# A sparse-attention and expert kernel: one small load moved ahead of K, three table loads moved to GpSimd's queue, one more unit transposed by TensorE

## The chip, the cores and the metric

The kernel runs on one core of a Trainium2 chip. The metric is the device time of one execution in microseconds (us). TensorE (PE) multiplies, VectorE (DVE) and ScalarE (ACT) do elementwise work, GpSimd (POOL) does elementwise work and issues gathers and scatters, and SyncE (SP) issues most transfers. Each engine takes its instructions strictly in the order of the program; the engines wait for one another by semaphores.

## What is computed

Block-sparse attention over 4 batches, 8 heads, 768 positions in 24 blocks of 32, followed by a mixture of 8 experts that gives each of the 3072 tokens to one expert:

```python
for qb in range(n_blocks):
    for kb in sampled_blocks[qb]:                 # 3 sampled blocks of a query block
        mask[qb*block:(qb+1)*block, kb*block:(kb+1)*block] = True   # beside window, first, last
attn = softmax(where(mask, q @ k.T / sqrt(D), -1e9));  x = attn @ v
e_idx = argmax(x @ w_gate, axis=1)                # the expert of each token
for e in range(E):
    mask = e_idx == e
    h  = np.maximum(x[mask] @ w1[e], 0.0)         # [*, 512] @ [512, 1024]
    out[mask] = gate_w[mask, None] * eom[mask, e, None] * (h @ w2[e])
```

## The kernel before

**Setup.** SP's queue opens with the two halves of K (`load_k`, L383), then six loads of V (L386). ACT's queue opens with the first tile of q and then `setup_load` (L184): the 72 sampled block numbers, broadcast to 128 partitions (`raw`). From `raw`, GpSimd marks repeated blocks (`setup_dup`, L217 to L227) and VectorE works out the gather indices `vidx` (`setup_blocks`, L314 to L351). VectorE's program has `setup_blocks` ahead of its first reduction over scores (`mx0d`, L563), GpSimd's has `setup_dup` ahead of the scaled copies of K (`fixed` L400, `gather_k` L422).

**Attention.** 52 units of work (4 dense and 22 sparse for each of two batch pairs) run as a software pipeline: in each step PE does the scores of one unit (L555 or L491), the transposes of another (L455), the output product of a third (L588 or L524 and L531).

**Experts.** Tokens are routed while attention still runs. Expert work is cut into units. Units 0 to 4 ("early") start before all tokens are known. Then a plan on VectorE and GpSimd (`plan`, L791 to L865) writes the table `es` with expert and first table row of the planned units, numbered from 5. Their kinds are, from unit 5 on, P P M P P M P M P M S S: P has 256 tokens, S 128, M 32. For each unit SP reads registers from `es` (`load_g`, L920 and L922), loads the unit's rows of the token table (`load_t`, L937 for M, L940 for P and S, which also waits for the 24 scatters that fill the table) and its weights in eight pieces of 512 KB (`load_w`, L948); GpSimd gathers the tokens (`load_x` L969, `m_load` L1107) and scatters results (`store_y`, L1095). Pieces live in three sets of buffers used in turn, so units 7 and 8 reuse those of units 4 and 5. A table tile is reused after four units, once the stores that read it have landed.

**Turning x.** PE needs x with the 512 features on partitions. For units in `PEX` (0 to 5) PE transposes it (L999), ACT writes the high half (L1000) and VectorE the low half (`x_l`, L1006). For the others ACT and VectorE split x first (`x_s`, L979 and L980), and SP's queue transposes it by DMA (L994).

**Order.** A hand-written schedule gives every piece of work a step and a rank inside it (`program`); the order of the ranks is the order on every engine. A step of the expert stage is about one group of 12 matmuls (L1045, `p_h`) and one of 6 (L1077, `p_y`). `first(u, j)` is the step from which piece j of unit u may be loaded. Unit 4 starts at step 32, unit 5 at 40, unit 6 at 48; unit 7 multiplies at steps 54 to 56, unit 8 starts at 56.

Of the kernel before, what the change touches and what calls it, by code (L numbers as in the profile page):

```python
# [15 lines left out]
ET = mybir.EngineType  # L16

B, H, S, D = 4, 8, 768, 64
NB, BLK = 24, 32
# [7 lines left out]
EMPTY = E * LS  # L27
# [6 lines left out]
NE = 5  # L34
NOWN = NE - 1
# [28 lines left out]
EARLY_X = (28, 29), (36, 36), (38, 39), (48, 49), (53, 54)  # L64
# [13 lines left out]
FIRST = PER + ND + 1  # L78
# [9 lines left out]

PEX = tuple(range(NE + 1))
PARTS = (5, 5, 4), (5, 5)

KC = (("act", 3, (0,)), ("pool", 3, (1, 2)), ("pool", 2, (3, 4, 5)))
# [18 lines left out]
def tile_kernel(ctx, tc, q, k, v, sampled, wg, wcat, out):  # L113
    nc = tc.nc
# [66 lines left out]

    def setup_load():
        src = sampled.bitcast(I32).rearrange("a c -> (a c)").rearrange("(o n two) -> o n two", o=1, two=2)
        nc.scalar.dma_start(raw, src.to_broadcast([128, NB * 3, 2]))  # L184

    setp = ExitStack()
    sp = setp.enter_context(tc.tile_pool(name="setup", bufs=1))
# [584 lines left out]
    def after_scatters(i, n=NT):  # L772
        for name in scattered[:n]:
            tc.add_manual_dep(
                i, name, mybir.DependencyInfo(mybir.DependencyClass.Sync, mybir.DependencyReason.DATA),
                reason="table")
# [140 lines left out]
    def load_g(u):  # L917

        w = u - NE
        _, regs[u] = nc.values_load_multi_w_load_instructions(  # L920
            es[w:w + 1, 0:2], engines=[ET.SP], min_val=0, max_val=E - 1)
        rows[u], = nc.values_load_multi_w_load_instructions(  # L922
            es[w:w + 1, 2:3], engines=[ET.SP], min_val=0, max_val=EMPTY)[1]

    def load_t(u):
        m = 1 if KIND[u] == "M" else 2
        tabs[u] = rt.tile([128, m, TW], I32, tag=f"tab{m}", name=f"tab{u}", bufs=4)
        m = tiles_of(u)
        if u < NE:
            src = table[ds(regs[u][1], 128 * m)].rearrange("(p m) c -> p m c", m=m)  # L930
            after_scatters(nc.sync.dma_start(tabs[u][:, 0:m], src).ins, RG[OF[u]][1])
            return
        assert len(scattered) == NT
        if KIND[u] == "M":

            src = table[ds(rows[u], 32)].rearrange("(o p) c -> o p c", o=1).to_broadcast([4, 32, TW])
            after_scatters(nc.sync.dma_start(tabs[u][:, 0], src).ins)  # L937
            return
        src = table[ds(rows[u], 128 * m)].rearrange("(p m) c -> p m c", m=m)
        after_scatters(nc.sync.dma_start(tabs[u][:, 0:m], src).ins)  # L940

    def load_w(n):
        u, j = n // 8, n % 8
# [324 lines left out]
    def program(n0, n1):  # L1268
# [13 lines left out]
        def first(u, j):  # L1282

            if u < NE + 2:
                return (30, 34)[u - NE] + j // 2
            v = u - 3
            return POS[v] + 1 + j // 4 if KIND[v] == "M" else POS[v] + j - 2

        for u in range(NUNIT):
            t = POS[u]  # L1290
            small = KIND[u] == "M"
            if u >= NE:
                later = end + u - NE
                get = max(min(t - 28, first(u, 0)), later)
                do(get, 0, load_g, u)
                for j in range(NFC):
                    do(max(first(u, j), get), 0.6, load_w, NFC * u + j)
                do(max(t - 18, later), 0.5, load_t, u)
            if small:
                do(max(t - 16, later + 1), 1, m_load, u)  # L1300

                for d, rank, f in ((-4, 9.5, m_x), (-3, 7.5, m_xc), (-2, 9.5, m_h), (-1, 7.5, m_hc), (-1, 9.5, m_t),
                                   (0, 7.5, m_tc), (0, 9.5, m_y), (1, 7.5, m_o), (2, 13, m_store)):
                    do(t + d, rank, f, u)
                continue
            if u >= NE:
                for m in range(2):
                    do(max(t - 16, later + 1), 1, load_x, 2 * u + m)
                do(max(t - 10, later + 3), 13, x_s, u)
            for m in range(2):  # L1310
                x = max(t - 2 + m, EARLY_X[u][m] + 1 - FIRST) if u < NE else t - 3 + m if u in PEX else t - 8
                do(x, 15, x_t, 2 * u + m)
                do(x + 1 if u < NE else x, 3 if u < NE else 16, x_l, 2 * u + m)
            yl = LAG(u, 7) + 1
            do(t + 7 + yl, 4 if u < NOWN else 12, y_o, u)
            for m in range(2):
                do(t + 8 + yl + (m if u < NOWN else 0), 13, store_y, 2 * u + m)
            e = u < NOWN
            lead = 2 if e else 3
            for j in range(NFC):  # L1320
                n, p = NFC * u + j, t + j
                do(p - lead, 6, w_h, n)
                do(p - lead, 7, w_l, n)
                if e:

                    do(max(p - 5, (-3, 5, 5, 15)[u]), 0.6, load_w, n)
                elif u < NE:
                    do(p - 10, 0.6, load_w, n)
                do(p, 8, p_h, n)
                do(p + LAG(u, j), 9, p_y, n)  # L1330
                if j % 2 == 1:
                    do(p if u < NE else p + 1, 10, h_h, n // 2)
                    do(p + 1, 2 if u < NE else 11, h_l, n // 2)
# [134 lines left out]
```

## Time and profile before

| | |
|---|---|
| median of three runs | 585.51 us (585.29 to 586.24) |
| the profiled execution | 588.49 us, its span 586.7 us |
| PE busy | 519.2 us (89% of the span), 7373 matmuls |
| DVE, ACT, POOL busy | 354.6, 314.2, 242.2 us |
| TensorE clock granted, mean | 0.956 of full speed |
| DMA | 138.67 MB, mean 236 GB/s |

PE is the busiest engine. The share is an average: it is near full in the second half of the expert stage and lower in the first 40 us and where the expert units follow one another around 370 to 430 us. In a row of the timeline the columns are start, duration, engine, line, operation, tiles, shapes and count; in brackets stands how long the engine was idle before it and what ended that. An engine's name with a q is its sequencer (SPq: a transfer is issued).

### The profile page before, as it was taken

The page shows a single profiled execution, that of the slowest core. Times are in us where ns is not written, and L with a number is a line of the kernel's source. Part 1 is how long each engine was busy: PE and PEld are TensorE (multiplying, and loading weights), DVE is VectorE, ACT ScalarE, POOL GpSimd, SP SyncE. Part 2 cuts the span into 40 slices and gives each one's busy share as a digit, 9 for nine tenths or more (in the row PEclk, how much of TensorE's full clock was granted, in tenths as well). Part 3 has the DMA queues.
Part 4 walks back from the last instruction along what each step waited for, and adds up shares of the span by engine and source line. Part 5 has one row for each costly group of instructions (what it writes and reads, how often), then busy time and mean ns, then how long its engine had stood idle before and what let it go on. Part 6 is the DMA issues. An engine that isn't in the chain of part 4 may idle for free. (4 is left out here: it accounts for less than half of the span.)

```text
span 586.7 us, 18727 instructions
## 1 busy us (share of the span) xinstructions
PE 519.2 (89%) x7373; PEld 361.5 (62%) x7373; DVE 354.6 (60%) x730; ACT 314.2 (54%) x583; POOL 242.2 (41%) x366
## 2 busy tenths in 40 slices
PE   4389889897888989999998999896899999999994
PEld 3157666565556657676765666574567666766772
DVE  2677657575657647776763567656366474555571
ACT  1165656565556647577674546355375455455470
POOL 2853644743560783817837007420322303312111
PEclk8599989999998989999999899898989999999998
DMA  8955979794398459776865376399998999976111
GB/s 313 305 169 187 331 228 302 229 324 110 79 298 274 143 172 336 237 223 198 254 196 194 94 286 235 139 384 408 287 347 309 299 405 312 288 245 221 24 39 35
DMA packets 60481, 138.67 MB, mean 236 GB/s; under 512 B 21663, under 2 KB 28319, under 8 KB 60128
## 3 DMA queue, kind: packets, MB, share of 16 engines
q1 hardware_dynamic: 48896, 100.57, 53.3%
q0 software_dynamic: 11200, 36.48, 20.1%
q8 instruction: 60, 0.98, 0.7%
q10 hardware_dynamic: 288, 0.34, 0.2%
q14 instruction: 37, 0.30, 0.2%
HBM read 128.05 MB, written 14.81 MB: 244 GB/s over the span
## 5 line engine op out<-in xcount | busy, mean ns | idle before, releaser
L1045 PE MATMUL h<-xb,kr 128*128 128x256 f16 (+1 forms) x780 | 90.7, 267 | 10.0 <-ACT xb L1000 4.8
L1045 PEld LDWEIGHTS <-kr 128*128 128x128 f16 x780 | 71.0, 100 | 30.7 <-issue 12.5
L1077 PE MATMUL S<-kr,hh 128*128 128x512 f16 x348 | 86.2, 382 | 0.0
L422 POOL TENSOR_TENSOR kr<-kn,eighth 128x256 f32<-128x256 f32 x110 | 68.5, 649 | 19.4 <-issue 9.4
L498 DVE TENSOR_REDUCE mx<-S 128x4 f32<-128x1024 f32 x44 | 53.7, 1221 | 35.4 <-PE S L491 19.2
L506 ACT ACTIVATE P<-S,mx 128x256 f32<-128x256 f32 x176 | 69.3, 483 | 9.4 <-DVE mx L498 6.5
L458 ACT COPY pt<-T 128x512 f32<-128x512 f32 x66 | 36.6, 589 | 46.4 <-PE T L455 41.8
L439 POOL DMA_INDIRECT vt<-in_v_dram,vidx x44 | 47.6, 1083 | 29.1 <-PE O L524 23.0
L1077 PEld LDWEIGHTS <-hh 128*128 128x128 f16 x384 | 37.3, 99 | 31.2 <-issue 1.2
L491 PE MATMUL S<-kr,qall 64*32 64x256 f32 x1408 | 50.9, 394 | 1.4 <-issue 1.4
L1058 ACT ACTIVATE hh<-h 128x512 f16<-128x512 f32 (+1 forms) x36 | 19.8, 549 | 60.4 <-PE h L1045 59.2
L1031 DVE SCALAR_TENSOR_TENSOR kr<-e,kr 128x1024 f16<-128x1024 f32 x32 | 38.7, 1226 | 19.1 <-ACT kr L1027 14.7
L455 PE MATMUL T<-ident,P 128*128 128x128 f32 x352 | 48.6, 281 | 0.7 <-issue 0.7
L455 PEld LDWEIGHTS T<-ident,P 128*128 128x128 f32 x352 | 41.7, 148 | 2.1 <-issue 1.4
L524 PE MATMUL O<-vt,pt 128*32 128x65 f32 x1408 | 34.5, 222 | 8.7 <-issue 8.3
L531 PE MATMUL O<-vc,pt 128*64 128x65 f32 x704 | 33.7, 229 | 6.6 <-issue 6.5
L969 POOL DMA_INDIRECT xb<-xscr,tab x16 | 16.4, 1027 | 53.6 <-PE O L1045 14.6
L765 POOL DMA_INDIRECT table<-vals,place x24 | 26.0, 1085 | 28.8 <-DVE vals L716 15.0
L524 PEld LDWEIGHTS O<-vt,pt 128*32 128x32 f32 x1408 | 26.5, 109 | 18.3 <-issue 12.9
L1064 DVE SCALAR_TENSOR_TENSOR hh<-h,hh 128x512 f16<-128x512 f32 (+1 forms) x36 | 22.6, 627 | 21.8 <-ACT hh L1058 21.8
L1095 POOL DMA_INDIRECT out_dram<-yo,tab x16 | 17.6, 1101 | 42.4 <-ACT yo L1088 33.9
L491 PEld LDWEIGHTS S<-kr,qall 64*32 64x32 f32 x1408 | 22.2, 108 | 19.8 <-issue 10.5
(342 smaller groups left out, 981.1 us busy)
## 6 DMA issues: line engine op xcount, KB each, us to landing
e<-in_wcat_dram SPq DMA_DIRECT2D x80, 512.0 KB
rk<-in_wcat_dram SPq DMA_DIRECT2D x30, 512.0 KB
vc<-in_wcat_dram SPq DMA_DIRECT2D x14, 512.0 KB
vn<-in_v_dram SPq DMA_DIRECT2D x12, 520.0 KB
xscr<-x SPq DMA_DIRECT2D x48, 128.0 KB
qall<-in_q_dram SPq DMA_DIRECT2D x23, 256.0 KB
vc<-in_v_dram SPq DMA_DIRECT2D x22, 260.0 KB
ws<-in_wcat_dram SPq DMA_DIRECT2D x8, 512.0 KB
```

What stands on the lines that cost most here:

```text
L422: nc.gpsimd.tensor_tensor(r[:, slot], kn[bp][:, ds(rv, 1)].rearrange("p o n -> p (o n)"), eighth.to_broadcast([128, 256]), op=ALU.mult)
L439: nc.gpsimd.indirect_dma_start(vt[bp, i][:, s].rearrange("p b j w -> p (b j w)"), None, v, bass.IndirectOffsetOnAxis(ap=vidx[:, bp, i, s:s ...
L455: nc.tensor.transpose(pt[:, 128 * c:128 * c + 128], p[:, 128 * c:128 * c + 128], ident)
L458: nc.scalar.copy(t[:, 0:w], pt[:, 0:w])
L491: nc.tensor.matmul(s[64 * h2 + 32 * qi:64 * h2 + 32 * qi + 32, b, hp], t[p, 64 * j + 32 * qi:64 * j + 32 * qi + 32], g[p, 1 - qi:3:1 + qi, ...
L498: nc.vector.tensor_reduce(mx, self.s.rearrange("p b h n -> p (b h) n"), axis=AX.X, op=ALU.max, negate=True)
L506: nc.scalar.activation(p[:, 256 * hp:256 * hp + 256], self.s[:, b, hp], AF.Exp, bias=self.mx[:, 2 * b + hp:2 * b + hp + 1])
L524: nc.tensor.matmul(o[row:row + 32, b, hp, 0:VW], self.t[b][:, col:col + 32], av[:, qi, b, 4 * h2 + 2 * hg + hp], start=b == 0 and hp == 0, ...
L531: nc.tensor.matmul(o[64 * h2:64 * h2 + 64, b, hp, 0:VW], self.t[b][:, col:col + 64], cv[:, b, 4 * h2 + 2 * hg + hp], start=False, stop=b = ...
L1031: nc.vector.scalar_tensor_tensor(w[:, 1], piece(n), SW, w[:, 0], op0=ALU.mult, op1=ALU.subtract)
L1045: nc.tensor.matmul(hps[n // 2][:, cols(n)], w[:, hl, 128 * c:128 * c + 128], x[:, xl, c], start=cnt == 0, stop=cnt == 11)
L1077: nc.tensor.matmul(y, a[:, k], w[:, l, 512:1024], start=n % 8 == 0 and cnt == 0, stop=n % 8 == 7 and cnt == 2)
```

## The change

`setup_load` moves from ACT's queue to SP's, where it stands ahead of the two loads of K. For units 5, 6 and 7 the first-row register is read on GpSimd and `load_t` is issued from GpSimd's queue. `PEX` takes in unit 6, so its x is transposed by PE and no longer split by `x_s` and transposed by DMA. `x_t` of unit 4 stands one step earlier (29 and 30 for its two halves), that of unit 5 one step later (38 and 39); unit 6's stands at 46 and 47. The pieces of unit 7 are loaded from steps 41 to 48 on (34 to 37 before), those of unit 8 from 43 to 50 (38 to 45 before).

```diff
+POOLT = NE + 3
-PEX = tuple(range(NE + 1))
+PEX = tuple(range(NE + 2))
 def setup_load():
-        nc.scalar.dma_start(raw, src.to_broadcast([128, NB * 3, 2]))
+        nc.sync.dma_start(raw, src.to_broadcast([128, NB * 3, 2]))
 def load_g(u):
-            es[w:w + 1, 2:3], engines=[ET.SP], min_val=0, max_val=EMPTY)[1]
+            es[w:w + 1, 2:3], engines=[ET.Pool if u < POOLT else ET.SP], min_val=0, max_val=EMPTY)[1]
 def load_t(u):
+        queue = nc.gpsimd if u < POOLT else nc.sync
-            after_scatters(nc.sync.dma_start(tabs[u][:, 0], src).ins)
+            after_scatters(queue.dma_start(tabs[u][:, 0], src).ins)
-        after_scatters(nc.sync.dma_start(tabs[u][:, 0:m], src).ins)
+        after_scatters(queue.dma_start(tabs[u][:, 0:m], src).ins)
 def first(u, j):
+            if u < NE + 4:
+                return (41, 43)[u - NE - 2] + j
 def program(n0, n1):
-                x = max(t - 2 + m, EARLY_X[u][m] + 1 - FIRST) if u < NE else t - 3 + m if u in PEX else t - 8
+                x = max(t - (2 if u < NOWN else 3) + m, EARLY_X[u][m] + 1 - FIRST) if u < NE else t - 2 + m if u in PEX else t - 8
```

## Rows read from the trace of the kernel before

**Rows 1.** Windows: length, busy PE, PEld, DVE, ACT, POOL, clock, DMA, GB/s.

```profile
400.00:420.00 20.00, 18.07 (x119) 12.14 (x119) 13.75 (x14) 11.87 (x16) 3.56 (x4) 0.91 1.05 369
480.00:500.00 20.00, 20.00 (x191) 13.79 (x190) 10.90 (x12) 12.13 (x17) 7.01 (x6) 1.00 1.03 312
```

**Rows 2.** Timeline of all engines, first 48 us.

```profile
0.74 0.90 SPq L383 DMA_DIRECT2D kn<-in_k_dram  x2
1.17 0.45 ACTq L184 DMA_DIRECT2D raw<-in_sampled_dram  x1
7.93 0.88 PE L555 MATMUL S<-kn,qall 64*64 64x384 f32 x8 [2.03 <-ACT qall L396]
12.86 0.19 DVE L314 COPY smp<-raw 1x72 int32<-1x72 int32 x1 [9.74 <-DMA raw<-in_sampled_dram]
13.33 1.56 PE L555 MATMUL S<-kn,qall 64*64 64x384 f32 x8 [4.52 <-DMA kn<-in_k_dram]
15.60 2.32 POOL L400 TENSOR_TENSOR kr<-kn,eighth 128x256 f32<-128x256 f32 x4
22.11 0.95 DVE L563 TENSOR_REDUCE mx0d<-S 128x1 f32<-128x768 f32 x1
24.20 3.77 PE L555 MATMUL S<-kn,qall 64*64 64x384 f32 x16 [9.32 <-ACT P01d L571]
47.60 1.21 POOL L422 TENSOR_TENSOR kr<-kn,eighth 128x256 f32<-128x256 f32 x2 [8.10 <-PE S L491]
```

**Rows 3.** Timeline of PE where unit 4 starts.

```profile
371.30 0.60 PE L999 MATMUL O<-ident,xb 128*128 128x128 f32 x4
374.68 2.50 PE L1045 MATMUL h<-xb,kr 128*128 128x256 f16 x11 [1.83 <-DVE xb L1006]
378.68 1.47 PE L1045 MATMUL h<-xb,kr 128*128 128x256 f16 x12
381.29 1.47 PE L1045 MATMUL h<-xb,kr 128*128 128x256 f16 x12
```

**Rows 4.** Timeline of DVE at the same place.

```profile
371.12 0.69 DVE L1006 SCALAR_TENSOR_TENSOR xb<-O,xb 128x512 f16<-128x512 f32 x1
```

**Rows 5.** Timeline of PE where units 5 and 6 start.

```profile
395.20 1.46 PE L1077 MATMUL S<-kr,hh 128*128 128x512 f16 x6
400.82 0.27 PE L1045 MATMUL h<-xb,kr 128*128 128x256 f16 x1 [4.16 <-ACT xb L1000]
406.10 1.47 PE L1045 MATMUL h<-xb,ws 128*128 128x256 f16 x12
421.74 1.46 PE L1077 MATMUL S<-kr,hh 128*128 128x512 f16 x6
425.46 2.63 PE L1045 MATMUL h<-xb,kr 128*128 128x256 f16 x12 [2.26 <-DMA xb<-xb]
429.73 1.47 PE L1045 MATMUL h<-xb,kr 128*128 128x256 f16 x12
```

**Rows 6.** Timeline of ACT around the starts of units 5 and 6.

```profile
399.23 1.06 ACT L979 ACTIVATE xb<-xb 128x1024 f16<-128x1024 f32 x1 [6.59 <-DMA xb<-xscr,tab]
400.19 0.58 ACT L1000 ACTIVATE xb<-O 128x512 f16<-128x512 f32 x1
425.19 1.06 ACT L979 ACTIVATE xb<-xb 128x1024 f16<-128x1024 f32 x1 [7.82 <-DMA xb<-xscr,tab]
```

**Rows 7.** Timeline of PE: an idle stretch and the group behind it.

```profile
347.95 0.40 PE L648 MATMUL lp<-fold,lt 128*128 128x16 f32 x2 [1.43 <-ACT lt L643]
348.20 1.47 PE L1045 MATMUL h<-e 128*128 128x256 f16 x12
```

**Rows 8.** Timelines of SP and POOL: a table load and two gathers.

```profile
377.94 0.98 POOL L969 DMA_INDIRECT xb<-xscr,tab  x1 [5.64 <-issue]
408.34 0.34 SPq L940 DMA_DIRECT2D tab<-table  x1
415.53 1.53 POOL L1107 DMA_INDIRECT mx<-xscr,tab  x1 [19.19 <-DMA tab<-table]
```

## The prediction, made before the changed kernel ran

> **What bounds the kernel now.** I read the chain of waits first: it stops in the last two stores and tells nothing of the middle. So I read the windows of busy time by stage, then PE's timeline where the windows are not full, and there the row that ended each wait. In the late expert stage PE is busy 20.00 of 20 us with the DMA engines as good as full beside it, while between 400 and 420 it lacks 2 us [rows 1]. PE sets the time, and what can be won lies in its holes. Two kinds are touched by the change.
>
> The first is the start. K is there at 13.33 and PE ends the first scores at 14.89, but the reduction that follows starts only at 22.11 [rows 2]. VectorE has the block numbers' setup ahead of it, and these numbers, issued at 1.17 from ACT's queue, are first used at 12.86, so the setup runs from 12.86 to the reduction without a pause worth naming. 22.11 - 14.89 = 7.2 us are lost behind a load of 72 KB.
>
> The second are the starts of units 4, 5 and 6. The undisturbed pace is one group of 12 and one of 6 in 381.29 - 378.68 = 2.61 us, 1.30 each [rows 3]. Unit 4: from the end of the transposes at 371.90 to 378.68 are 6.78 us for one such pair, so 4.2 lost; the wait ends with VectorE's low half of x. Unit 5: from 395.20 to 406.10 are 10.9 us for three groups (3.9), so 7.0 lost; without the loss it would start at 396.5. Unit 6: from 421.74 to 429.73 are 8.0 us for three groups, so 4.1 lost, and the wait is for the DMA transpose [rows 5]. These sums hold the half-speed matmuls after each hole: 11 of them took 2.50 us where 12 take 1.47 [rows 3].
>
> **The change part by part.** The sum is made against the profiled execution, 588.5 us (span 586.7), 3.0 us or 0.5% above the median of 585.5; I take the same microseconds off the median.
>
> *Block numbers ahead of K.* Two loads of K issued together at 0.74 are used at 7.93 and at 13.33 [rows 2]: one queue is served in order, so what stands first in it lands first. With 72 KB against 3 MB I expect the numbers by about 4 us. Setup takes 22.11 - 12.86 = 9.3 us, so it ends by 13.3 at the latest, before PE's first scores at 14.89, and sooner because GpSimd's copies, which started at 15.60, still wait for K. K leaves up to one issue later, 0.45 us. The reduction then starts at about 15.2: 22.11 - 15.2 = 6.9 us gained. What is late next? GpSimd's copies start with K, some 2 us sooner than now; they need not be 7 sooner, since GpSimd stands idle 8.10 us before 47.60, waiting for PE. The bounds are 5 and 9: the 16 matmuls at 24.20 took 3.77 where 8 take 0.88 at the full level [rows 2], so 2.0 us hang on when the clock comes back, earlier or later. The steps behind depend on one another, not on the hour, so the gain goes through attention to the plan.
>
> *Unit 4's x one step earlier.* Its second low half moves ahead of the plan's last operations on VectorE, to where the first half's stood, 371.12 to 371.81 [rows 4]. PE would come to it at 371.90 [rows 3]. Of 4.2 lost I keep 0.2: gain 4.0. If the half-clock stretch came all the same, 2.5 is the low bound, 4.2 the high.
>
> *Unit 6 in PEX.* In ACT's order unit 6's `x_s` stood ahead of unit 5's second half. It waited 6.59 us for its gather, until 399.23, and unit 5's half followed at 400.19 [rows 6]. That `x_s` goes, and with it ACT 1.06 us and VectorE's like; both did not bound. But unit 5's own transposes now stand one step later, directly ahead of its first group: transposes 0.60, ACT 0.58, VectorE 0.69 [rows 3, 4, 6] and handoffs follow one another there, and PE has nothing else in its queue. Beyond the 0.4 us that transposes cost PE anyway that is a hole of about 1.5 us. An idle stretch of 1.43 us was followed by a group of 12 at the usual 1.47 [rows 7], so I take no clock loss; with one it is 1.2 us more. Unit 5: 7.0 - 1.5 = 5.5 gained (bounds 3.2 and 7.0).
>
> Unit 6 gets the same hole of 1.5 and eight transposes that PE did not do before, 1.0 us at most by 0.60 for four. 4.1 - 2.5 = 1.6. One thing is queued ahead of it on ACT: unit 8's `x_s` in the same step, which now waits 7.82 us, until 425.19, for a gather that hangs on SP's table load at 408.34 [rows 6, 8]. Eight pieces of unit 7 that went ahead of that load now come behind it: 8 x 0.524 MB at 369 GB/s [rows 1] are 11 us, and SP issues three table loads fewer, another 1 to 2. So that gather lands near 412.5, and PE comes to unit 6 near 423 - 4.0 - 5.5 = 413.5. It is close; I charge 0.5. Unit 6: 1.1 gained (bounds -1.5 and 4.0).
>
> *Table rows from GpSimd's queue.* Three register reads and three issues, about 1 us each by its gathers, in time where GpSimd idles (5.64 us before 377.94, 19.19 before 415.53) [rows 8]. Behind them stand the gathers of units 5 and 6 and the stores of unit 3. Unit 5's gathers may start 1 to 2 us later, since unit 6's load now stands ahead of them. From a table load to the end of its gathers the longest that the rows show is 408.34 to 425.19, 16.9 us [rows 6, 8]; from about 376, 2 us before the gather at 377.94, that ends at 393, and PE wants the x at 396.5 - 4.0 = 392.5. Zero, with 2 us to pay if it is late: that is in unit 5's low bound. The Trainium skill's "DMA: Bandwidth & Descriptors" (Issuing engine by pattern; Specifications) speaks against this part: a plain load belongs to Sync, about 0.6 us to the first byte against 1 us from GpSimd. No row shows a plain load from GpSimd; by that page the sum would be 0.4 us smaller at most.
>
> *Weights of units 7 and 8 later.* The bytes stay, the DMA engines are full from here on [rows 1], so unit 6's pieces come sooner and unit 7's later. Zero, while the queue stays full.
>
> **Sum:** 6.9 + 4.0 + 5.5 + 1.1 = 17.5 us. 588.5 - 17.5 = 571.0 for an execution like the profiled one, 585.5 - 17.5 = **568.0** for the median. All low bounds together give 9.2, all high ones 24.2; since they hardly come together I take 12 to 22 for this case, 563.5 to 573.5.
>
> **The rivals.** *Numbers land with K.* If the load shares the DMA engines with K wherever it is queued, it still comes near 12.9 and the start stays: 585.5 - 10.6 = 574.9. For it: 11.7 us from issue to use though it is small. Against it: the order of the two K loads [rows 2]. Chance 0.05. Beside it stands a rule of the same page (Queues, rings and completion order): an engine drains a packet of some 9 to 17 descriptors from one queue before it turns to another, by which so small a load is not held up by K in either place and moving it brings nothing. The trace speaks against the rule: the numbers came 5 us after the q ahead of them on their own queue.
>
> *Weights starve PE.* PE would use 10.6 us less from 370 on, and the DMA engines have no room [rows 1]. If they bound, the three starts are given back later and only the start's gain stays: 578.6. Twelve units of eight pieces are 50.3 MB, at 312 to 369 GB/s 136 to 161 us from about 376, so to 512 to 537; the last unit's eight steps are at most 21 us, so its last piece is wanted no sooner than 586.7 - 17.5 - 21 = 548. That speaks against it; chance 0.10.
>
> *ACT stands again.* Unit 8's gather comes 4 us later than I make it and unit 6 starts as late as before: about 572. Chance 0.12, inside the range.
>
> *The table rows are slow from GpSimd (slower than before).* GpSimd works in order, so a late table row holds its gathers and with them unit 5's first group. A table row has kept it waiting 19.19 us [rows 8]. Every microsecond beyond the slack is one of PE's. Unit 5's x is wanted 392.5 - 376 = 16.5 us after its row can be asked for, and gathers take 425.19 - 415.53 = 9.7 until they have landed [rows 6, 8], so the row has 6.8. The gains being 17.5, it decides from 24.3 us on; at 27 us the time is 585.5 + 2.7 = 588.2. Against it: the row that was asked for from an empty queue held its gather at 377.94 for some 2 us only. Chance 0.03.
>
> **How the numbers follow.** My case 0.68, ACT 0.12, weights 0.10, numbers 0.05, slow rows 0.03, others 0.02. The ends of the range, 561.5 and 576.0, take in most of my case, ACT's and the numbers'. About 0.2% or 1.2 us is what a measurement of this kernel tells from no change: faster 0.95, the same 0.02, slower 0.03.
>
> **What would show it.** After the change: VectorE's first use of the numbers near 4 us; the reduction at L563 near 15 in place of 22.11, with K's second scores still near 13.3; no `x_s` and no DMA transpose of unit 6; in PE's timeline, all some 7 us earlier, holes of about 0.2, 1.5 and 1.5 to 2 us at the starts of units 4, 5 and 6; from there full windows. I am wrong if the reduction stays behind the numbers, if a hole over 3 us stands before unit 5 or 6, or if PE waits for weights after unit 6.

## The result, and the profile after

| | before | after |
|---|---|---|
| median, side by side | 585.40 us | 577.05 us (575.45 to 577.50) |
| ratio after/before | | 0.9853, 95% interval 0.9828 to 0.9879 |
| profiled execution, span | 588.49, 586.7 us | 575.45, 573.8 us |
| PE busy | 519.2 us | 516.7 us |
| mean TensorE clock | 0.956 | 0.962 |

The change is faster by 8.35 us, 1.4%. The forecast was 17.5 us and a range that ended at 576.0; the measured 577.05 lies 1 us outside it. A median here is that of all executions of a kernel, while a ratio and its interval leave out the executions counted as slow against the fastest of the same kernel, the profiled ones of before and of xs8_later among them, so a ratio is not always the quotient of its two medians. The two profiled executions differ by 12.9 us in span, more than the medians: the one of before lay 3 us above its median, the one of after 1.6 us below its own.

In the changed kernel a line of code stands two or three lines lower than in before (L563 is now L565, L1000 is L1003). The first view is the timeline of all engines at the start: start, duration, engine, line, operation, tiles, shapes, count, and in brackets the idle time before it and what ended that.

```profile
0.86 0.41 SPq L186 DMA_DIRECT2D raw<-in_sampled_dram  x1
1.33 0.91 SPq L385 DMA_DIRECT2D kn<-in_k_dram  x2
6.59 0.19 DVE L316 COPY smp<-raw 1x72 int32<-1x72 int32 x1 [3.35 <-DMA raw<-in_sampled_dram]
10.34 1.56 PE L557 MATMUL S<-kn,qall 64*64 64x384 f32 x8 [5.17 <-DMA kn<-in_k_dram]
...
13.95 1.56 PE L557 MATMUL S<-kn,qall 64*64 64x384 f32 x8 [2.05 <-DMA kn<-in_k_dram]
...
15.56 0.96 DVE L565 TENSOR_REDUCE mx0d<-S 128x1 f32<-128x768 f32 x1 [2.83 <-PE S L557]
```

Against [rows 2]: the numbers are used at 6.59 instead of 12.86, and the reduction stands at 15.56 instead of 22.11. It now waits for PE's scores, and these for K. The scores on K's first half start 2.4 us later than before (10.34 for 7.93), and K itself comes at least that much later, since at 7.93 they waited for q and not for K. Those on the second half, which wait for K in both kernels, start 0.6 us later (13.95 for 13.33).

The second view is PE's timeline where units 4, 5 and 6 start.

```profile
361.45 0.60 PE L1002 MATMUL O<-ident,xb 128*128 128x128 f32 x4
...
364.50 1.47 PE L1048 MATMUL h<-xb,kr 128*128 128x256 f16 x12
365.81 1.74 PE L1080 MATMUL S<-ws,e 128*128 128x512 f16 x6
367.38 1.47 PE L1048 MATMUL h<-xb,kr 128*128 128x256 f16 x12
...
386.05 0.27 PE L1048 MATMUL h<-xb,kr 128*128 128x256 f16 x1 [0.69 <-ACT xb L1003]
386.77 1.36 PE L1048 MATMUL h<-xb,kr 128*128 128x256 f16 x11 [0.46 <-DVE xb L1009]
387.97 1.46 PE L1080 MATMUL S<-kr,hh 128*128 128x512 f16 x6
389.27 1.47 PE L1048 MATMUL h<-xb,ws 128*128 128x256 f16 x12
...
406.64 0.60 PE L1002 MATMUL O<-ident,xb 128*128 128x128 f32 x4
409.48 0.27 PE L1048 MATMUL h<-xb,kr 128*128 128x256 f16 x1 [2.24 <-ACT xb L1003]
411.15 2.51 PE L1048 MATMUL h<-xb,kr 128*128 128x256 f16 x11 [1.40 <-DVE xb L1009]
413.45 2.77 PE L1080 MATMUL S<-kr,hh 128*128 128x512 f16 x6
416.01 2.00 PE L1048 MATMUL h<-xb,kr 128*128 128x256 f16 x12
```

Unit 4 starts without a hole, and its second group, at 367.38, stands 11.3 us ahead of the 378.68 of [rows 3]. Unit 5 has 0.69 + 0.46 us of waiting at the full clock; its second group, at 389.27, is 16.8 us ahead of the 406.10 of [rows 5]. At unit 6 there are 2.24 + 1.40 us, then matmuls at half speed, and its second group, at 416.01, is only 13.7 us ahead of 429.73: 3.1 us are given back.

The third view is the timeline of all engines around that hole, without PE and VectorE.

```profile
388.13 0.33 SPq L943 DMA_DIRECT2D tab<-table  x1
...
398.09 0.99 POOL L972 DMA_INDIRECT xb<-xscr,tab  x1 [8.85 <-DMA tab<-table]
...
406.45 1.06 ACT L982 ACTIVATE xb<-xb 128x1024 f16<-128x1024 f32 x1 [5.75 <-DMA xb<-xscr,tab]
407.42 0.58 ACT L1003 ACTIVATE xb<-O 128x512 f16<-128x512 f32 x1
...
407.89 1.05 ACT L1030 ACTIVATE kr<-e 128x1024 f16<-128x1024 f32 x1
...
408.84 0.59 ACT L1003 ACTIVATE xb<-O 128x512 f16<-128x512 f32 x1
```

It is read from below. PE waits for the second L1003, ACT's half of unit 6's x. ACT could not do it sooner, since it stood 5.75 us in L982, the split of unit 8's x, and then had four pieces of work in a row to catch up with. The split waited for its gather, the gather (398.09) for the table row, and that row left SP's queue at 388.13.

### The profile page after: what moved, and what is told of

Same layout as the page of the kernel before. It is cut to its first block, busy times and chain, and to the rows that moved or that the text cites. A ratio compares the mean times of both kernels' runs of the same rounds, so it can differ in the third digit from the quotient of the medians.

```text
span 573.8 us, 18734 instructions
## 1 busy us (share of the span) xinstructions
PE 516.7 (90%) x7381; PEld 360.2 (63%) x7381; DVE 352.7 (61%) x731; ACT 314.3 (55%) x584; POOL 245.4 (43%) x369
## 5 line engine op out<-in xcount | busy, mean ns | idle before, releaser
L1048 PE MATMUL h<-xb,kr 128*128 128x256 f16 (+1 forms) x780 | 88.7, 264 | 4.8 <-ACT xb L1003 2.9
L1080 PE MATMUL S<-kr,hh 128*128 128x512 f16 x348 | 86.7, 383 | 0.0
L1048 PEld LDWEIGHTS <-kr 128*128 128x128 f16 x780 | 70.4, 99 | 24.3 <-issue 7.2
L441 POOL DMA_INDIRECT vt<-in_v_dram,vidx x44 | 49.1, 1117 | 28.0 <-PE O L526 21.9
L1080 PEld LDWEIGHTS <-hh 128*128 128x128 f16 x384 | 37.2, 99 | 31.2 <-issue 1.1
L1061 ACT ACTIVATE hh<-h 128x512 f16<-128x512 f32 (+1 forms) x36 | 19.8, 550 | 58.5 <-PE h L1048 51.5
L972 POOL DMA_INDIRECT xb<-xscr,tab x16 | 20.0, 1249 | 50.4 <-DMA tab<-table 30.9
L526 PEld LDWEIGHTS O<-vt,pt 128*32 128x32 f32 x1408 | 26.8, 110 | 17.6 <-issue 12.9
L533 PEld LDWEIGHTS O<-vc,pt 128*64 128x64 f32 x704 | 26.3, 139 | 12.0 <-issue 8.2
```

The source lines that it names most:

```text
L441: nc.gpsimd.indirect_dma_start(vt[bp, i][:, s].rearrange("p b j w -> p (b j w)"), None, v, bass.IndirectOffsetOnAxis(ap=vidx[:, bp, i, s:s ...
L526: nc.tensor.matmul(o[row:row + 32, b, hp, 0:VW], self.t[b][:, col:col + 32], av[:, qi, b, 4 * h2 + 2 * hg + hp], start=b == 0 and hp == 0, ...
L533: nc.tensor.matmul(o[64 * h2:64 * h2 + 64, b, hp, 0:VW], self.t[b][:, col:col + 64], cv[:, b, 4 * h2 + 2 * hg + hp], start=False, stop=b = ...
L1048: nc.tensor.matmul(hps[n // 2][:, cols(n)], w[:, hl, 128 * c:128 * c + 128], x[:, xl, c], start=cnt == 0, stop=cnt == 11)
L1080: nc.tensor.matmul(y, a[:, k], w[:, l, 512:1024], start=n % 8 == 0 and cnt == 0, stop=n % 8 == 7 and cnt == 2)
```

## The experiments

The kernel before took 566 to 589 us, depending on the chip, so each kernel is compared by its ratio to the kernel before on the same chip. Beside the ratio I cut each profile into stretches by the starts of PE's matmul groups; all these kernels have the same number of them (1248 matmuls of L1045/L1048). The *mark* is the start of four matmuls of L1077/L1080 that follow a wait of about 1.1 us some ten microseconds ahead of unit 4 (362.15 in before, 354.93 in after). "Unit 4" runs from there to the start of that unit's second full group (378.68 in before), "unit 5" from there to 406.10, "unit 6" to 429.73, "rest" to the end of the span. What lies ahead of the mark is attention and routing, and it varies: the two kernels of the last pair below, which are alike up to there, reached the mark at 340.15 and at 347.42.

| kernel | median, of before | ratio (95% interval) | unit 4 | unit 5 | unit 6 | rest | mark to end |
|---|---|---|---|---|---|---|---|
| before | | | 16.53 | 27.41 | 23.64 | 156.92 | 224.50 |
| b_again | 565.61, 567.18 | 0.9976 (0.9936 to 1.0016) | 15.02 | 29.84 | 19.76 | 154.96 | 219.58 |
| raw_only | 582.68, 588.55 | 0.9904 (0.9870 to 0.9939) | 16.70 | 28.26 | 19.55 | 158.69 | 223.20 |
| raw_only_2 | 559.48, 566.24 | 0.9912 (0.9873 to 0.9950) | 16.70 | 27.44 | 20.06 | 153.81 | 218.01 |
| after | 577.05, 585.40 | 0.9853 (0.9828 to 0.9879) | 12.45 | 21.88 | 26.75 | 157.78 | 218.86 |
| a_again | 578.59, 588.55 | 0.9861 (0.9812 to 0.9909) | 12.44 | 21.88 | 27.74 | 157.11 | 219.17 |
| a_again_2 | 563.25, 566.24 | 0.9936 (0.9895 to 0.9977) | 12.45 | 21.88 | 27.39 | 154.49 | 216.21 |
| a_again_3 | 561.14, 566.09 | 0.9842 (0.9775 to 0.9909) | 12.44 | 21.88 | 28.13 | 156.43 | 218.88 |
| no_raw | 586.62, 588.55 | 0.9986 (0.9940 to 1.0032) | 12.44 | 21.88 | 27.12 | 157.31 | 218.75 |
| no_raw_2 | 567.41, 567.18 | 1.0006 (0.9966 to 1.0046) | 12.44 | 21.88 | 27.90 | 159.52 | 221.74 |
| no_pool | 559.59, 566.24 | 0.9886 (0.9838 to 0.9933) | 12.44 | 21.88 | 29.01 | 155.95 | 219.28 |
| no_late_w | 567.10, 567.67 | 0.9991 (0.9945 to 1.0036) | 12.44 | 21.88 | 37.02 | 155.69 | 227.03 |
| poolt4 | 577.62, 588.55 | 0.9807 (0.9754 to 0.9861) | 12.44 | 21.88 | 21.88 | 161.21 | 217.41 |
| xs8_later | 563.71, 567.18 | 0.9909 (0.9865 to 0.9953) | 12.45 | 21.88 | 21.88 | 167.74 | 223.95 |
| p4_xs8 | 561.29, 567.18 | 0.9880 (0.9821 to 0.9940) | 12.44 | 21.88 | 21.88 | 161.72 | 217.92 |
| xs_all | 559.42, 567.67 | 0.9880 (0.9823 to 0.9936) | 12.44 | 21.88 | 21.88 | 164.47 | 220.67 |
| pool_all | 556.66, 567.67 | 0.9831 (0.9768 to 0.9894) | 12.45 | 21.88 | 21.88 | 156.56 | 212.77 |
| pool_all_2 | 554.78, 566.24 | 0.9820 (0.9781 to 0.9859) | 12.45 | 21.88 | 22.07 | 160.84 | 217.24 |
| pool_all_3 | 559.78, 566.09 | 0.9873 (0.9826 to 0.9920) | 12.44 | 21.88 | 21.88 | 157.25 | 213.45 |
| pool_xs | 556.48, 567.67 | 0.9777 (0.9698 to 0.9856) | 12.45 | 21.88 | 21.88 | 158.43 | 214.64 |

### The two halves of the change

raw_only is before with the edit of `setup_load` alone; no_raw is after without it.

```diff
 # raw_only
-        nc.scalar.dma_start(raw, src.to_broadcast([128, NB * 3, 2]))
+        nc.sync.dma_start(raw, src.to_broadcast([128, NB * 3, 2]))
 # no_raw
-        nc.sync.dma_start(raw, src.to_broadcast([128, NB * 3, 2]))
+        nc.scalar.dma_start(raw, src.to_broadcast([128, NB * 3, 2]))
```

> The kernel before with one part of the change: the block numbers go ahead of K in SyncE's queue, the expert stage is untouched. Theory A (the start's gain goes through, less what half-clock stretches and holes in attention take back): the reduction at L563 starts near 15.6 instead of 22.1 us, and the time falls by 4 to 6 us, to about 580. Prediction on record: 6.9 us, 578.6. Theory B (most of the gain is given back before the expert stage): 0.5 to 2 us, about 584.

> The changed kernel with the block numbers back on ScalarE's queue, so only the expert stage is changed. Theory A: units 4 and 5 give 4.1 + 5.5 us, unit 6 takes 3.1 back, so 3 to 6.5 us under the kernel before, 579 to 582. Theory B (the holes of the profiled execution of before at units 4 to 6 are larger than usual, and their gain is mostly not there in the median; the start carries the result): 0 to 2.5 us, about 584. If both parts are independent, the gains of this kernel and of the start alone add up to the 8.35 us of the whole change.

The start alone gives 0.9904, the expert stage alone 0.9986. The first is 5.6 us of 585.4 and theory A; the second is 0.8 us and theory B, although no_raw's own profile shows units 4 and 5 as short as in after. I took the second figure for an unlucky sample, and ran it again beside the kernel before.

> The same kernel as no_raw (the expert stage changed, the start not), timed once more, because its first ratio of 0.9986 lies 3 us above what its own profile shows: from the wait at L1077/L1080 in front of unit 4 to the end it takes 219.8 us where the kernel before takes 225.7. Theory A (the gains add, the first figure was an unlucky sample of attention, where half-clock stretches come and go): 3.5 to 6 us under the kernel before, ratio 0.990 to 0.994, and again 219 to 221 us from that wait to the end. Theory B (the expert stage's gain is not there in a typical execution): ratio 0.997 to 1.000.

> The kernel before once more, unaltered, for a second profile of its expert stage. Theory A: the holes in front of units 4, 5 and 6 are again near 2.5, 5.3 and 2.3 us and from the wait at L1077 in front of unit 4 to the end 224 to 226 us pass; the ratio is 1.00. Theory B: the holes sum to under 7 us, or the stretch is shorter than 222 us.

1.0006: theory A of the expert stage fell. b_again shows half of why, and is theory B with 219.58 us from the mark to the end. Its holes stand at units 4 and 5 as in before (that of unit 5 is 5.63 + 1.01 us instead of 4.16 + 1.11), but at unit 6 there is none. Of the four profiles with the old expert stage only the one that the prediction was read from has it: unit 6 took 23.64 there and 19.55 to 20.06 in the others. PE's timeline of raw_only_2 shows the usual picture (unit 5's two waits, then the 0.35 us that are left of unit 6's):

```profile
378.42 0.27 PE L1045 MATMUL h<-xb,kr 128*128 128x256 f16 x1 [4.05 <-ACT xb L1000]
379.80 2.51 PE L1045 MATMUL h<-xb,kr 128*128 128x256 f16 x11 [1.11 <-DVE xb L1006]
401.29 1.47 PE L1045 MATMUL h<-xb,kr 128*128 128x256 f16 x12 [0.35 <-DMA xb<-xb]
```

### The whole change again

> The changed kernel once more, unaltered, for a second profiled execution. Theory A (the two profiled executions shown lay on opposite sides of their medians, 3.0 us above and 1.6 us below): time 576 to 578, the profiled execution within 1.5 us of that, and the same holes at the starts of units 4 to 6 as in the first profile, with half-clock stretches at other places or of other length. Theory B (the holes themselves change from execution to execution): the holes before units 5 and 6 differ by over 1 us from 0.5 and 3.6.

The ratio is that of the first measurement, and what is left of the holes at units 4 and 5 goes with theory A; the time, 578.59, lies 0.6 us over that theory's range. Unit 6's hole, 3.43 + 1.31 us, is longer by over 1 us than the 2.24 + 1.40 of the first profile, which is theory B there. In all four profiles of the changed kernel the hole at unit 4 is gone, that at unit 5 is down to 0.7 + 0.5 us, and the third stands: unit 6 takes 26.75 to 28.13 us. Beside raw_only_2 on one chip:

> The changed kernel, unaltered, beside the next three on one chip. Theory F (late table rows on SyncE's queue make ScalarE stand and take 4 to 8 us of the expert stage's gain back): ratio 0.984 to 0.990; in the profile 219 to 223 us from the wait in front of unit 4 to the end, with holes of 3 us or more in front of unit 6 or of L1136 or of a later unit. Rival: the ratio is 0.980 or less and no such hole shows.

> The kernel before with the start alone changed, beside the whole change on the same chip. Theory A: ratio 0.988 to 0.992, 4.5 to 6.5 us. If the expert stage adds a typical 2 to 4 us, a_again_2 lies that much under it; if it adds nothing, both are level within 1.5 us.

a_again_2's ratio and its 216.21 us from the mark to the end both lie outside what was expected of it, the hole in front of unit 6 (3.77 + 1.41 us) inside. 0.9936 for the whole change and 0.9912 for its start alone: on that chip the expert stage added nothing that can be told from zero. On the chip of raw_only (0.9904) and a_again (0.9861) it added about 0.4%, with intervals that overlap.

### Who holds unit 6

poolt4 takes unit 8's table row out of SP's queue too; xs8_later moves the split of unit 8's x behind unit 6's halves on ACT; p4_xs8 does both.

```diff
 # poolt4, p4_xs8
-POOLT = NE + 3
+POOLT = NE + 4
 # xs8_later, p4_xs8
-                do(max(t - 10, later + 3), 13, x_s, u)
+                do(max(t - 10, later + 3) + (2 if u == NE + 3 else 0), 13, x_s, u)
```

> The changed kernel with one number changed: the table row of unit 8 also comes from GpSimd's queue, ahead of the gathers of unit 5, and no longer from SyncE behind the wait for unit 3's stores. Theory C (unit 6 starts late because ScalarE stands in the split of unit 8's x, which waits for a gather that hangs on this table load): that wait of 5.75 us falls below 3, the hole in front of unit 6 shrinks from 2.2 + 1.4 us to about 1.5, and the time is 2 to 4 us under the changed kernel. Rival D (the hole is the chain TensorE, ScalarE, VectorE, TensorE by itself, or the row waits for the same stores on GpSimd's queue and holds the gathers behind it): the same time within 1 us, or 1 to 5 us slower with a longer hole in front of unit 5.

> The changed kernel with one thing moved: the split of unit 8's x stands two steps later on ScalarE and VectorE, behind unit 6's two halves; its table row and gather stay as they are. Theory C (unit 6's hole is ScalarE's wait for that gather): the hole in front of unit 6 falls from 2.2 + 1.4 us to about 0.7 + 0.5, and the time by 2 to 3.5 us, to 574 to 576 by the first measurement. Rival D (the hole comes from the chain of transposes, copies and matmuls itself, or unit 8 then starts late by what unit 6 wins): within 1 us of the changed kernel, with a new hole in front of unit 8.

> Both edits on the changed kernel: unit 8's table row from GpSimd's queue and the split of unit 8's x two steps later. Theory C: ScalarE no longer waits in front of unit 6 at all; one of the two is enough, so the time is that of poolt4 or xs8_later within 1.5 us. Rival E (the weights are next: after the holes are gone the small units' weights come late, as in poolt4's profile, where TensorE pauses 1.8 us inside L1126 and 1.7 us after it near 482 to 490 us): the time gains nothing more and pauses of 2 to 5 us stand inside L1126.

Each of them closes the hole: unit 6 takes 21.88 us, as unit 5 does. The timeline of poolt4, ACT and PE:

```profile
409.76 1.06 ACT L982 ACTIVATE xb<-xb 128x1024 f16<-128x1024 f32 x1 [3.09 <-DMA xb<-xscr,tab]
410.73 0.58 ACT L1003 ACTIVATE xb<-O 128x512 f16<-128x512 f32 x1
...
413.46 0.60 ACT L1003 ACTIVATE xb<-O 128x512 f16<-128x512 f32 x1 [1.21 <-PE O L1002]
...
414.11 0.27 PE L1048 MATMUL h<-xb,kr 128*128 128x256 f16 x1 [0.69 <-ACT xb L1003]
414.83 1.36 PE L1048 MATMUL h<-xb,kr 128*128 128x256 f16 x11 [0.46 <-DVE xb L1009]
```

ACT stands 3.09 us instead of 5.75, has caught up before the second L1003, and waits 1.21 us for PE there; PE waits only the 0.69 + 0.46 us of unit 5's kind. So theory C holds for unit 6's hole.

The row of unit 8 does not leave earlier for it. The timeline of poolt4, GpSimd:

```profile
394.68 0.58 POOL L943 DMA_DIRECT2D tab<-table  x1 [7.38 <-DMA out_dram<-e,tab]
...
400.51 1.25 POOL L972 DMA_INDIRECT xb<-xscr,tab  x1 [3.95 <-issue]
```

From the mark the row leaves at 33.6 us (mark 361.13), in after at 33.2 (388.13). But the gather that needs it starts 5.8 us behind it and no longer waits for it, in after 10.0 us behind it and because of it.

For the time theory C is not borne out. poolt4 is 1 us under a_again by the medians (577.62 and 578.59); the ratios are 0.9807 and 0.9861, with intervals that overlap. xs8_later is at 0.9909 and p4_xs8 at 0.9880, on a chip on which the changed kernel was not run. The rest, 154 to 158 us in after's profiles, is 161.2 and 161.7 in poolt4 and p4_xs8. What PE wins at unit 6 it waits for further on: PE's pauses in the rest sum to 0.8 us in after, 3.8 in poolt4 and 4.6 in p4_xs8. The timeline of p4_xs8:

```profile
470.30 1.06 ACT L982 ACTIVATE xb<-xb 128x1024 f16<-128x1024 f32 x1 [10.17 <-DMA xb<-xscr,tab]
...
472.21 0.36 ACT L1132 ACTIVATE mh<-O 128x256 f32<-128x256 f32 x1
472.63 0.69 PE L1136 MATMUL O<-ident,mh 128*128 128x128 f32 x2 [4.63 <-ACT mh L1132]
```

It is the same thing a second time: ACT stands 10.17 us in the split of a later unit's x (unit 13, by the order of the program), and the small unit 10, whose `mh` comes behind it on ACT, keeps PE waiting 4.63 us. The pauses inside L1126 that rival E asked for are not in p4_xs8.

### Later splits, earlier rows, earlier weights

```diff
 # xs_all, pool_xs
-                do(max(t - 10, later + 3), 13, x_s, u)
+                do(max(t - 8, later + 3), 13, x_s, u)
 # pool_all, pool_xs
-POOLT = NE + 3
+POOLT = NE + 99
 # no_pool
-POOLT = NE + 3
+POOLT = NE
 # no_late_w
-            if u < NE + 4:
-                return (41, 43)[u - NE - 2] + j
```

> The changed kernel with the split of x of every later planned unit two steps (5.2 us) later on ScalarE and VectorE; transposes, gathers and table rows keep their places. Theory F (what the first starts win is given back later in the same way as at unit 6: ScalarE, in order, stands in the split of some later unit's x behind a late gather, for up to 13 us, and TensorE runs dry): the holes in front of unit 6 and in front of L1136 fall below 1 us each, the wait in front of unit 4 to the end takes 214 to 217 us, and the time is 3 to 6 us under the changed kernel, ratio 0.976 to 0.981. Rival G (the DMA engines are full, so a later split only moves the wait to the transposes behind it): within 1.5 us of the changed kernel, ratio 0.984 to 0.989, holes of the same sum that end with DMA.

> The changed kernel with the table rows of all planned units issued from GpSimd's queue, none from SyncE's, where a row lands some 8 us after its issue behind pieces of weights. Theory F: rows land 2 to 4 us after issue, gathers start 4 us sooner, no hole over 1 us in front of unit 6 and of L1136, 2 to 5 us under the changed kernel. Rival H (GpSimd works in order, so a row that waits for the stores of four units before holds the gathers behind it): holes of 2 to 8 us in front of later units, 0 to 6 us slower than the changed kernel.

> Both edits together. Theory F: the longer slack of both adds, no hole over 0.7 us from unit 6 to the last unit, 5 to 7 us under the changed kernel, ratio 0.974 to 0.978. Rival G: the sum of pauses from unit 6 on stays over 4 us, ended by DMA, ratio over 0.982.

> The changed kernel with the weights of units 7 and 8 loaded as early as before. Forecast on record: zero difference while the queue stays full. Theory F: the pieces of unit 7 stand ahead of the table row of unit 8 again, so that row lands some 5 us later, ScalarE stands longer in front of unit 6 and the time is 2 to 5 us over the changed kernel. Rival W (loading them later is what makes weights and gathers late after 440 us): 1 to 4 us under the changed kernel, with no hole in front of L1136.

**xs_all** shows that ACT's place in the order is not the root. With all splits two steps later unit 6 is closed, but near 470 us PE waits for the transposes of the x that came late instead, and the rest takes 164.5 us. That is rival G. The timeline of xs_all:

```profile
470.60 1.65 PE L1048 MATMUL h<-xb,kr 128*128 128x256 f16 x7 [5.21 <-DMA xb<-xb]
470.71 1.06 ACT L982 ACTIVATE xb<-xb 128x1024 f16<-128x1024 f32 x1 [6.20 <-DMA xb<-xscr,tab]
```

**no_late_w** brings unit 7's and 8's weights forward again, and unit 6 takes 37.02 us, 9.5 more than the 27.5 that the changed kernel's four profiles give on average; it is level with the kernel before. Theory F was right in kind and too low in size. Its timeline:

```profile
378.90 0.33 SPq L943 DMA_DIRECT2D tab<-table  x1
388.67 0.98 POOL L972 DMA_INDIRECT xb<-xscr,tab  x1 [18.84 <-DMA tab<-table]
...
396.39 1.06 ACT L982 ACTIVATE xb<-xb 128x1024 f16<-128x1024 f32 x1 [16.43 <-DMA xb<-xscr,tab]
...
399.41 0.37 PE L1048 MATMUL h<-xb,kr 128*128 128x256 f16 x1 [12.71 <-ACT xb L1003]
```

**pool_all** closes unit 6 and leaves the rest at 156.6: 212.8 us from the mark to the end, 6 below after. I set it beside the changed kernel on two more chips, on the first of them with no_pool too.

> All planned table rows from GpSimd's queue, beside the changed kernel on the same chip. Theory F: 3 to 7 us under a_again_2, ratio to the kernel before 0.975 to 0.982, 213 to 216 us from the wait in front of unit 4 to the end, no hole over 1 us behind it. Rival (the first profile was a lucky one): within 1.5 us of a_again_2.

> The changed kernel with all planned table rows on SyncE's queue, as before. Forecast on record: zero, with 2 us to pay in either direction at unit 5. Theory F: the rows of units 5 and 6 land later behind the weights, the hole in front of unit 5 grows from 0.7 to 3 us or more or that in front of unit 6 stays, and the time is 1 to 5 us over a_again_2. Rival (the rows lie off the path, what helps units 5 and 6 is the order of weights and transposes): within 1 us of a_again_2.

> The changed kernel, unaltered, beside all rows on GpSimd's queue. Theory F: ratio 0.984 to 0.994 and 216 to 222 us from the wait in front of unit 4 to the end, with a hole of 3 to 5.5 us in two parts in front of unit 6.

> All planned table rows from GpSimd's queue, beside a_again_3. Theory F (late rows cost the changed kernel 3 us or more): ratio at least 0.005 below that of a_again_3, 212 to 217 us from the wait in front of unit 4 to the end, and 0.7 + 0.5 us in front of unit 6. Rival (the lead on the chip before came from attention, which differs from execution to execution): within 0.003 of a_again_3's ratio.

The two pairs contradict each other in time: 0.9820 against 0.9936, as theory F has it, then 0.9873 against 0.9842, where it asked for at least 0.005 less. Behind the mark pool_all takes 212.77, 217.24 and 213.45 us, on average 214.5, and the changed kernel 216.21 to 219.17, on average 218.3. So the rows give 3.8 us behind the mark on average, while the worst of the first lies over the best of the second (pool_all_2, at 217.24 over the 216 expected of it, waits 2.68 us for a DMA transpose of x at 462.75), and what of it is left in the time of an execution was not settled, because attention varies by more than that. pool_xs has the lowest ratio of all, 0.9777, with an interval (0.9698 to 0.9856) that holds two of pool_all's three figures, and one pause of 1.36 us behind unit 6, but it was not run beside the changed kernel. I don't call either shown to be faster than the change.

What pool_all alters is seen when the rows of units 12 and 13 leave. The timeline of a_again_3, SP:

```profile
450.96 0.72 SPq L940 DMA_DIRECT2D tab<-table  x1
452.03 0.35 SPq L943 DMA_DIRECT2D tab<-table  x1
```

The timeline of pool_all_3, GpSimd:

```profile
399.50 0.58 POOL L943 DMA_DIRECT2D tab<-table  x1 [6.71 <-DMA out_dram<-yo,tab]
...
440.37 0.77 POOL L940 DMA_DIRECT2D tab<-table  x1
448.17 0.58 POOL L943 DMA_DIRECT2D tab<-table  x1 [7.02 <-DMA tab<-table]
```

The rows of units 12 and 13 are the last two of each. From the mark they are 110.8 and 111.9 us on SP (mark 340.15) and 93.0 and 100.8 us on GpSimd (mark 347.42): 11 to 18 us sooner, for rows of the same step in the program. 6.3 us of this are PE's own delay at unit 6 (28.13 for 21.88). In poolt4, whose unit 6 has no hole either, the two leave SP at 108.4 and 109.5 us from the mark, 9 to 15 us later than from GpSimd. The waits of SP's queue name what it stands in (columns: engine, line, what it waited for, us in total, times, the longest). Three of a_again_3's, 340 to 520 us:

```profile
SPq L943 <- DMA out_dram<-yo,tab: 12.5, 3, 9.0
SPq L997 <- DVE xb L983: 7.0, 1, 7.0
SPq L997 <- PE h L1048: 6.8, 2, 5.5
```

The first are table rows that wait for the stores that still read their tile, the others transposes that wait for a split or a free tile; weights and later rows stand behind both. In pool_all the first wait is GpSimd's (6.71 us in front of the row at 399.50), and PE did not wait for what stands behind it there. The rows did not land as soon as expected (2 to 4 us): those of 16 KB took 5.3 us (median of six).

**no_pool** answers for the part of the change that put three rows there. Unit 5 takes 21.88 us without it as with it, and unit 6 29.01 for 27.50 on average. Beside a_again_2 it is not slower (0.9886 and 0.9936, with intervals that overlap; by the medians 3.7 us faster). Theory F asked for 1 to 5 us more and missed; the rival, the rows of units 5 to 7 lie off the path, has it but for the 1.5 us at unit 6 of this one profile, and its 1 us of time was missed on the fast side.

## Why the forecast failed

**The start was right.** Forecast 6.9 us, the reduction near 15.2; it stands at 15.56, 6.55 us sooner. Numbers were to be there at about 4 and are used at 6.59, which costs nothing, since the setup still ends ahead of PE's scores. In time the start gives 0.9904 and 0.9912, on average 5.4 us of 585.4; 6.9 us would be 0.9882, inside both intervals. The rival *numbers land with K* is out.

What held the numbers up shows in the DMA packets of the trace. In before their 128 rows of 576 bytes start only at 6.79, behind those of q on ACT's queue (1.78 to 6.41), and last until 12.05; in the same 5.3 us start 128 of K's rows of 12 KB on SP's queue, one for each row of the numbers. In after they run from 2.09 to 6.14, and K's first row starts at 4.10. By the Trainium skill's "DMA: Bandwidth & Descriptors" (Queues, rings and completion order) an engine drains a packet of some 9 to 17 descriptors from one queue before it turns to the next. The trace does not agree: spread evenly, 128 rows are eight for each of the 16 engines, and they took turns about one for one with K's. No run sets the numbers ahead of q on ACT's queue, so the queue and the place in it are told apart by these packets alone.

**Unit 4 was right.** Forecast 4.0: 16.53 became 12.45, 4.1 gained. Against the average of the four old profiles, 16.24, it is 3.8.

**Unit 5 was right.** Forecast 5.5: 27.41 became 21.88, 5.5, and against the old average of 28.24 it is 6.4. The hole of 1.5 that I charged is 0.69 + 0.46, without a half-clock stretch, as assumed. That the rows from GpSimd cost nothing there is right too (no_pool).

**Unit 6 is the step that failed, in two terms.** It reads: 4.1 lost before, less 1.5 for the hole, 1.0 for eight transposes and 0.5 for ACT, 1.1 gained.

The price of ACT was mis-sized: it was 4.9 to 6.3 us instead of 0.5. Where ACT is not in the way, unit 6 takes 21.88 (poolt4, p4_xs8, pool_all), 1.8 below the 23.64 of before: the 4.1 - 2.5 = 1.6 of the step is confirmed. With ACT in the way it takes 26.75 to 28.13, and 21.88 from these is the price. I had set the landing of the gather (412.5) against PE's coming to unit 6 (413.5) and called it close. In after the split starts at 406.45 and PE runs dry at 407.24, so the landing was nearly in time; in the three other profiles the split starts 0.4 to 0.8 us after PE runs dry. What I left out is that ACT does not stand free when it lands. The split itself (1.06), the first half of unit 6 (0.58), a weight piece (1.05) and the second half (0.59) come one after the other [third view of after], and then VectorE with the same backlog, and after that hole PE ran at half speed (2.51 us for 11 matmuls). Of the 4.9 us in after 2.5 are the longer hole (3.64 us for 1.15), and 2.4 are the half speed of the 17 matmuls behind it (4.86 us from 411.15 to 416.01, where unit 5's take 2.50).

The other term is the 4.1 us lost before. It is in the profiled execution, but not in the three other profiles with the old expert stage, whose unit 6 takes 19.8 us on average. Against these the change makes unit 6 7.7 us longer, 2.1 of which the transposes and the hole of unit 5's kind would cost anyway (21.88 - 19.8).

A price of 0.5 for ACT would not have been kept either. Where unit 6's hole is closed and only that (poolt4, p4_xs8), the rest takes 161.2 and 161.7 us against 156.1 in the old profiles: 5 us that the forecast had at zero when it let every gain go through to the end, with full windows behind unit 6.

**"The same microseconds off the median" failed with it.** The profiled execution of before lay 3.0 us above the median, and I gave the median a gain from a hole of 3.9 us (23.64 - 19.8) that three of the four profiles don't have. On the average of the four profiles each the change takes 221.3 - 218.3 = 3.0 us from the expert stage, where 10.6 were forecast: unit 4 +3.8, unit 5 +6.4, unit 6 -6.75, the rest -0.4. With 5.4 from the start that is 8.4 us; 8.35 were measured. That they meet so closely is luck: the old profiles lie between 218.0 and 224.5, and in time the expert stage alone gave 0.8 us (no_raw) and nothing (no_raw_2), not 3.0.

**Weights of units 7 and 8, "zero", only holds inside the sum.** Taking that hunk away costs 9.5 us at unit 6. The prediction had this under unit 6, where eight pieces that no longer go ahead of unit 8's row were 11 us, and that estimate is right: from the mark the row leaves SP at 44.5 us in no_late_w (378.90, mark 334.41) and at 33.2 in after. Without the hunk the expert stage is longer than in the kernel before (227.0 us from the mark to the end against 221.3 on average), so it carries the rest of the expert stage's change.

**The rivals.** *ACT stands again* is what happened, in each of the profiles of the changed kernel; I gave it 0.12 and 572, because I priced it as "unit 6 starts as late as before" by the one profile. *Weights starve PE* gave 578.6, nearest to the 577.05, for the reason that the gains of the expert stage are given back further on. That part occurred, but only where unit 6's hole was closed by itself, and the waits whose end is seen end with x's gathers and transposes, not with weights; for 2.1 of poolt4's 3.8 us, inside L1126, the trace doesn't show what ended them, so late weights stay possible there. After's own windows behind the hole are full or nearly so:

```profile
400.00:420.00 20.00, 16.36 (x94) 10.32 (x93) 9.95 (x12) 8.84 (x12) 5.22 (x5) 0.83 0.82 306
420.00:440.00 20.00, 20.00 (x190) 13.56 (x188) 11.51 (x12) 10.87 (x15) 2.00 (x2) 1.00 1.07 347
480.00:500.00 20.00, 19.20 (x212) 13.12 (x202) 10.85 (x13) 10.49 (x14) 4.83 (x5) 1.00 0.83 279
```

(Windows of after: length, busy PE, PEld, DVE, ACT, POOL, clock, DMA share, GB/s; the first is the one with the hole, in before 18.07 us and clock 0.91 [rows 1].) *Slow table rows from GpSimd* was not seen, and pool_all, with all rows there, is the nearest to its opposite. The Trainium skill speaks against that queue in "DMA: Bandwidth & Descriptors" (Issuing engine by pattern; Issuing engines are not separate DMA queues): a plain load belongs to Sync, and a second issuing engine saves only the time to issue. Here the rows of units 12 and 13 left GpSimd 9 to 15 us sooner than SP, which takes its instructions in order and was standing in other waits. And unit 8's row, which left no sooner, was there in under 6 us instead of 10.0. The saving is not the issue but the place in the queue, that of SP's instructions and that of its transfers.

What stays open: whether the 3.8 us of pool_all behind the mark reach the time of an execution, and why the whole change came out at 0.9842 to 0.9861 in three comparisons and at 0.9936 in a fourth, on another chip, and how much of the expert stage's 3.0 us an execution keeps, since no_raw and no_raw_2 show at most 0.8.

## What to carry to other kernels

Before a hole in one profile is booked as a gain, look whether it stands in a second profile of the same kernel: unit 6's 3.9 us did not, while the holes at units 4 and 5 stood each time. When an engine works in order, price its late arrival as the wait plus everything that is queued behind it until it has caught up, and ask that of every later unit that goes through the same door, because closing one hole moves the arrival of the next one forward. Small transfers that others hang on should not stand in a queue whose head waits for something else; where such a queue runs behind its plan is read from the step at which it issues, and what its transfers wait for from the time between a row's issue and the gather that needs it.

## What the runs showed of the hardware

- The same kernel took 588.55 us on one chip and 566 to 568 us on four others. Within one chip, attention, in which the kernels compared were alike, reached the mark 7 us apart in two executions (340.15 and 347.42).
- With 72 KB ahead of K on K's queue, K's first row started 2.0 us later (2.12 to 4.10) and the scores on its second half 0.6 us later (13.33 to 13.95).
- Two queues took turns about one row for one: while the numbers' 128 rows of 576 bytes went out on ACT's queue (6.79 to 12.05 in before), 128 rows of K, 12 KB each, started on SP's.
- The holes of 0.69 + 0.46 us in front of units 5 and 6 were followed by matmuls at the full clock; in pool_all_3 the granted clock is 1.00 in each 20 us window from 400 to 500. The hole of 2.24 + 1.40 us was followed by a stretch at 0.5 (11 matmuls in 2.51 us), and its window has 0.83.
- A row of 16 KB from GpSimd landed 5.3 us after its issue in pool_all (median of six); SP's row at 388.13 in after, with eight pieces of weights issued in the 11.4 us before it, let its gather start 10.0 us later; SP's row at 409.19, with nothing issued on that queue since 399.52, let it start after 2.4 us.
